# Attention scores and products with v: one TensorE block for eight heads instead of two for four, from tile 6 on

## The chip, the cores and the metric

The kernel runs on one NeuronCore of a Trainium2 chip. The metric is the device time of one execution in microseconds (us); the times shown are medians of several executions. The five engines are TensorE (PE in the profile), VectorE (DVE), ScalarE (ACT), GpSimd (POOL) and SyncE (SP, which issues the DMAs). The profile splits TensorE in two rows: PE for the matmuls and PEld for the loads of the stationary operand.

## What is computed

Three layers follow each other. The first is attention over a sliding window, the other two are dense layers on its 2304 tokens:

```python
# q, k, v: (4 batches, 8 heads, 576 positions, 64)
scores = q @ k.T / sqrt(64)
scores = where(0 <= rel < 128, scores + bias, -1e9)   # rel = position of query - position of key
attn = exp(scores - max); attn = attn / (sum + 1e-9)
x = attn @ v                       # then reshaped to (2304 tokens, 512)
g = x @ w_gate                     # 512 x 1536
x = (silu(g) * (x @ w_val)) @ w_out
h = x @ w_in                       # 512 x 2048
out = silu(h) @ w_out2             # 2304 x 512
```

The sizes are fp32. Products of the dense layers are made of a high and a low part per operand (three passes in the format `float32r` each); the products with v are done in plain fp32.

## The kernel before, in words

**Tiles and parts.** The 2304 tokens are 18 tiles of 128. Six tiles are a part, so there are three parts: tiles 0 to 5, 6 to 11, 12 to 17. For each part the kernel runs attention, then the first dense layer (`moe1`, six groups of hidden columns), then the second (`moe2`, eight groups). The attention of part 1 is spread in time over the dense layers of part 0, and that of part 2 over those of part 1 (`spread`, `attention_part`); part 2's dense layers run without attention beside them. Attention of part 0 fills the start.

**Attention of one tile.** A tile has eight heads, handled in two halves (`hf` 0 and 1) of four heads. For each half `prepare` transposes k and q on TensorE (L398, L406) and splits each into a high and a low part (tiles KR and qt). Then `attend` runs this chain: the scores on TensorE (`score`, L448) into two PSUM banks, where the two 64-row halves of the array work on a bank each; masks (L464) and bias with a row minimum (L471) on VectorE; the exponential on ScalarE (L477); the inverse of the sum on VectorE (L493, L494); the normalization on GpSimd (L497); four transposes on TensorE (L515); a copy out of PSUM (L301, tile u); two selections on GpSimd that part the weights into those of the previous tile of keys (u, L529) and those of the tile's own (l, L522); the product with v on TensorE (`weigh`, L541), whose matmuls use 64 columns of the array each; and a copy into XST (parts 1 and 2) or a split into XOP (part 0). The first tile of a batch that begins at a tile's edge (tiles 0 and 9) has only its own keys: its scores are half as wide and its product with v has half as many matmuls.

**PSUM.** There are eight banks. A group of the dense layers holds three of them as accumulators X, Y and Z while its seven products run (`quad`, L762 to L764), and blocks of the output products (`out1`, L906 to L908, and `out2`, L936 to L938) hold one each until VectorE has added it to ACC (L920, L948).

**The order.** Every operation is put into a `Plan` with a cost in ns and a due time, and `Plan.issue` simulates the engines and writes out one fixed order for each. An engine of the plan takes, of the operations whose inputs are ready, the one with the earliest due time for which enough banks are free; it does not hold banks back for an operation that needs several. Limits by kind cap the banks in use: "mm" for dense layers, "B" for operands, "S" for scores, "C" for the transposed weights, "O" for products with v, "T" for transposed k and q, "att" for the last four together. On the chip each engine then runs its list strictly in order, and waits where an input is late. `at(x)` is the due time of tile x, about 24 us apart in parts 1 and 2; the scores of a half are due at `at(i + 0.5 * hf)`, its second pair of heads and its product with v a quarter of a tile later.

**Rings.** qt has two slots (one per half), u two, l one, c two, the loaded v three (a tile's product reads the v of the tile before it too).

Of the kernel before, what the change touches and what calls it, by code (L numbers as in the profile page):

```python
# [9 lines left out]
F32 = mybir.dt.float32  # L10
# [7 lines left out]
ALU = mybir.AluOpType  # L18
PSUM = bass.MemoryType.PSUM

P = 128
# [180 lines left out]
def attention_moe_moe2_kernel(  # L202
# [33 lines left out]
    nc = tc.nc  # L236
# [7 lines left out]
    N = BT * P  # L244
    NP = H // 2
    G1, G2 = F1 // (2 * P), F2 // (2 * P)
    NU, NO, NRAW, NW, NH, NTMP = 17, 3, 2, 3, 6, 8

    big = ctx.enter_context(tc.tile_pool(name="big", bufs=1))
# [3 lines left out]
    def ring(n, shape, dtype, name):  # L253
        return [big.tile(shape, dtype, name=f"{name}{i}") for i in range(n)]
# [23 lines left out]
    QT_R = ring(2, [P, 2, 2, P], F32R, "qt")  # L278
    C_R = ring(2, [P, 4, P], F32, "c")
    ST_R = ring(2, [P, 3, 4], F32, "st")  # L280
    U_R = ring(2, [P, 4, P], F32, "u")
    L_R = ring(1, [P, 4, P], F32, "l")
    BANKS = [psp.tile([P, 512], F32, name=f"bank{i}") for i in range(8)]
    KEPT = {
        "wg": drp.tile([2 * G1, P, DM], F32, name="kept_wg"),
# [5 lines left out]
        "o2": drp.tile([2 * G2, P, 2 * DM], F32, name="kept_o2"),  # L291
    }

    plan = Plan(BANKS, {"mm": 6, "att": 4, "T": 1, "S": 3, "C": 2, "O": 1, "B": 4})

    def cost(kind, n):
        a, b = COST[kind]
# [55 lines left out]
    def first(i):  # L353
        return (i * P) % S == 0
# [66 lines left out]
        plan.add("act", cost("act_ps", 256), due, q_hi, [bq], [qk])  # L421
        plan.add("dve", cost("dve", 256), due, q_lo, [bq], [qk], give=bq)

    def attend(i, hf, dues):
        n = 2 * i + hf
        qt, qk = QT_R[n % len(QT_R)], ("qt", n % len(QT_R))
        s = i % 2
        c = 0 if first(i) else s
        cs, us, ls = n % len(C_R), n % len(U_R), n % len(L_R)
        t, st, u, lo = C_R[cs], ST_R[cs], U_R[us], L_R[ls]  # L430
        uk, lk = ("uu", us), ("l", ls)
        heads = slice(4 * hf, 4 * hf + 4)

        banks = [Bank("S"), Bank("S")]

        def score():
            for p in range(2):
                for x, y in ((0, 0), (0, 1), (1, 0)):  # L440
                    for e in range(2):
                        rows = slice(64 * e, 64 * e + 64)
                        view = banks[e].tile.rearrange("p (a b c) -> p a b c", a=2, b=2)
                        rhs = KR[rows, y, 2 * hf + p]
                        dst = view[:, p]
                        if first(i):
                            rhs, dst = rhs[:, s], dst[:, 0]
                        nc.tensor.matmul(  # L448
                            dst, qt[rows, x, p, :], rhs, start=(x == 0 and y == 0), stop=(x == 1)
                        )  # L450

        reads = [qk, ("KR", s, hf)] + ([] if first(i) else [("KR", 1 - s, hf)])
        plan.add("pe", 6 * 118 + 60, dues[0], score, reads, banks, take=tuple(banks))

        def scores(e, due):
            bank = banks[e]
            ck, stk = ("c", cs, e), ("st", cs, e)
            view = lambda: bank.tile.rearrange("p (a b c) -> p a b c", a=2, b=2)
            cur = lambda: view()[:, :, c, :]
            prev = lambda: view()[:, :, 1 - c, :]  # L460

            def mask(m, src, port):
                plan.add(
                    "dve", cost("dve", 256), due, lambda: nc.vector.copy_predicated(cur(), m, src()), [], [bank],  # L464
                    port=port,
                )

            def biased():
                for p in range(2):
                    l = 2 * p + e  # L470
                    nc.vector.tensor_tensor_reduce(  # L471
                        t[:, l, :], cur()[:, p, :], alibi[:, 4 * hf + l, :], 1.0, HUGE, ALU.add, ALU.min, st[:, 0, l:l + 1]
                    )

            def exponent():
                for l in (e, 2 + e):
                    nc.scalar.activation(  # L477
                        t[:, l, :], t[:, l, :], AF.Exp, bias=st[:, 0, l:l + 1], scale=-1.0, accum_out=st[:, 1, l:l + 1]
                    )

            mask(m_up, (lambda: bigt) if first(i) else prev, first(i))
            if not first(i) and (crossing(i) or crossing(i - 1)):
                mask(m_cross if crossing(i) else m_after, lambda: bigt, True)
            plan.add("dve", 2 * cost("dve", 136), due, biased, [bank], [ck, stk], give=bank)
            plan.add("act", 2 * (cost("act", 128) + 186), due, exponent, [], [ck, stk])

        def normalized(ps, due):
            l = slice(2 * ps[0], 2 * ps[-1] + 2)
            nl = 2 * len(ps)
            cks, stks = [("c", cs, p) for p in ps], [("st", cs, p) for p in ps]  # L490

            def invert():
                nc.vector.tensor_scalar(st[:, 2, l], st[:, 1, l], 1e-9, None, ALU.add)  # L493
                nc.vector.reciprocal(st[:, 2, l], st[:, 2, l])  # L494

            def normalize():
                nc.gpsimd.tensor_tensor(  # L497
                    t[:, l], t[:, l], st[:, 2, l].rearrange("p (a b) -> p a b", b=1).to_broadcast([P, nl, P]), ALU.mult
                )

            plan.add("dve", 290, due, invert, [], stks, port=True)
            plan.add("pool", 64 + 2.0 * nl * P, due, normalize, stks, cks)

        for e in range(2):
            scores(e, dues[e])
        normalized((0, 1), dues[1])

        due = dues[1]
        cb, ob = Bank("C"), Bank("O")
        cps = lambda: cb.tile.rearrange("p (a b) -> p a b", b=P)  # L510
        ops = lambda: ob.tile[:, 0:2 * P].rearrange("p (a b) -> p a b", b=P)

        def turn():
            for l in range(4):
                nc.tensor.transpose(cps()[:, l, :], t[:, l, :], ident)  # L515

        plan.add("pe", 4 * 109, due, turn, [("c", cs, 0), ("c", cs, 1), "ident"], [cb], take=cb)
        copy_op(512, due, lambda: u, cps, [cb], [uk], give=cb)
        if not first(i):
            plan.add(  # L520
                "pool", cost("select", 512), due,
                lambda: nc.gpsimd.affine_select(  # L522
                    lo, u, [[0, 4], [1, P]], ALU.is_ge, 0.0, base=0, channel_multiplier=-1
                ),
                [uk], [lk],
            )
            plan.add(
                "pool", cost("select", 512), due,
                lambda: nc.gpsimd.affine_select(  # L529
                    u, u, [[0, 4], [-1, P]], ALU.is_gt, 0.0, base=0, channel_multiplier=1  # L530
                ),
                [], [uk],
            )
        parts = [(i, u)] if first(i) else [(i - 1, u), (i, lo)]

        def weigh():
            for p in range(2):
                for a, (tl, m) in enumerate(parts):
                    for j in range(2):
                        l = 2 * p + j  # L540
                        nc.tensor.matmul(  # L541
                            ops()[64 * j:64 * j + 64, p, :],
                            VLD_R[tl % len(VLD_R)][:, 4 * hf + l, :],
                            m[:, l, :],
                            start=(a == 0),
                            stop=(a == len(parts) - 1),
                        )

        reads = [uk] + ([] if first(i) else [lk]) + [x for tl, _ in parts for x in loaded(tl, "v", hf)]
        plan.add("pe", 540 * len(parts) + 60, due, weigh, reads, [ob], take=ob)  # L550
        ti = i % PT
        xt = XST[:, ti, 2 * hf:2 * hf + 2, :]
        xk = [("xt", ti, 2 * hf + p) for p in range(2)]
        if i >= PT:
            copy_op(256, due, lambda: xt, ops, [ob], xk, give=ob)
        else:
            slot, t0 = x_slot(hf, ti // BT), (ti % BT) * P
            xh, xl = XOP[:, slot, 0, :, t0:t0 + P], XOP[:, slot, 1, :, t0:t0 + P]
            keys = [("X", slot, kk, ti % BT) for kk in range(2)]
            copy_op(256, due, lambda: xh, ops, [ob], keys)  # L560
            plan.add(
                "dve", cost("dve", 256), due,
                lambda: nc.vector.tensor_tensor(xl, ops(), xh.bitcast(F32), ALU.subtract), [ob], keys, give=ob,  # L563
            )


# [399 lines left out]
    def attention_part(part, at):  # L966
        for i in range(part * PT, part * PT + PT):
            load(i, "k", at(i) - 14820.0)
            load(i, "q", at(i) - 20070.0)
            load(i, "v", at(i) - 7670.0)  # L970
            for hf in range(2):
                prepare(i, hf, at(i + 0.5 * hf) - 8000.0)
                attend(i, hf, [at(i + p / NP) for p in (2 * hf, 2 * hf + 1)])

    def ramp(x):
        return 5000.0 + 6130.0 * min(x, 1) + 10170.0 * min(max(x - 1, 0), 1) + 7700.0 * max(x - 2, 0)
# [124 lines left out]
```

## Time and profile before

| | |
|---|---|
| median of 3 executions | 954.29 us (953.21 to 955.04) |
| profiled execution | 954.24 us, span of its instructions 952.5 us |
| TensorE, matmuls | busy 931.7 us, 98% |
| VectorE, ScalarE, GpSimd | busy 68%, 52%, 37% |
| mean granted TensorE clock | 0.998 of 2.4 GHz |

The profile's times are us from the first instruction of that execution; the 1.7 us between span and time lie outside of it. Matmuls overlap: one record's duration is a latency, and what a matmul costs the engine is the distance between its start and the start of the next one. A name such as "L448" is a line of the kernel; one matmul instruction in plain fp32 shows as two records (L541).

### The profile page before, as it was taken

How to read it: one execution, taken by the hardware profiler on the slowest of the kernel's cores; microseconds unless marked ns; L12 is line 12 of the kernel's file. 1: busy time of each engine (PE TensorE's matmuls, PEld its weight loads, DVE VectorE, ACT ScalarE, POOL GpSimd, SP SyncE). 2: the span in 40 equal slices, each digit the busy share in tenths (PEclk: the TensorE clock that was granted, in tenths of full speed). 3: DMA queues.
4: the chain of work that ended last, by engine and by line, in shares of the span. 5: the costliest groups of instructions: out<-in, count | busy, mean ns of one | idle time of the engine just before them, and what ended most of it. 6: DMA issues, size and time to landing. Idle time of an engine off the chain costs nothing.

```text
span 952.5 us, 16827 instructions
## 1 busy us (share of the span) xinstructions
PE 931.7 (98%) x5662; PEld 854.8 (90%) x5662; DVE 644.8 (68%) x1489; ACT 499.2 (52%) x1269; POOL 352.9 (37%) x426
## 2 busy tenths in 40 slices
PE   7999999998999999999999999999999999999998
PEld 5888989998887888999999998888899999988886
DVE  7886666758798889557666756657745555855655
ACT  6877555556866765665453564345343323553331
POOL 2645333347666788796651521111200000300000
PEclk9999999999999999999999999999999999999999
DMA  9978897776578987998766666355466666654522
GB/s 216 276 240 253 271 301 260 256 241 207 189 255 262 293 266 259 362 285 287 227 200 185 198 201 191 125 167 184 162 239 201 208 214 215 204 198 170 161 89 89
DMA packets 156854, 209.78 MB, mean 220 GB/s; under 512 B 65760, under 2 KB 86496, under 8 KB 156768
## 3 DMA queue, kind: packets, MB, share of 16 engines
q1 hardware_dynamic: 156768, 208.71, 68.2%
q8 instruction: 45, 0.74, 0.3%
q14 instruction: 41, 0.34, 0.1%
HBM read 146.28 MB, written 62.39 MB: 219 GB/s over the span
## 4 chain that ended last, share of the span: by engine, by line
PE 86%; DVE 7%; DMA 3%; ACT 2%; POOL 1%; issue 1%; SPq 0%; DVEq 0%; ACTq 0%; POOLq 0%
PE bank L762 15%; PE bank L763 14%; PE bank L764 14%; PE bank L936 6%; PE bank L938 6%; PE bank L937 6%; PE bank L906 5%; PE bank L907 5%; PE bank L908 5%; PE bank L448 3%; PE bank L541 3%; DVE word L663 2%; PE bank L515 1%; DMA raw<-in_moe_w_in_dram 1%; DVE bank L464 1%
## 5 line engine op out<-in xcount | busy, mean ns | idle before, releaser
L762 PE MATMUL bank<-XOP,wu 128*128 128x384 f32 (+2 forms) x880 | 301.5, 343 | 6.7 <-DVE qt L412 2.1
L763 PE MATMUL bank<-XOP,wu 128*128 128x384 f32 (+2 forms) x880 | 293.8, 334 | 0.6 <-DVE XOP L563 0.5
L764 PE MATMUL bank<-XOP,wu 128*128 128x384 f32 (+2 forms) x880 | 294.0, 334 | 0.1
L762 PEld LDWEIGHTS bank<-XOP,wu 128*128 128x128 f32 x880 | 165.5, 188 | 15.9 <-ACT tmp L301 2.8
L763 PEld LDWEIGHTS bank<-XOP,wu 128*128 128x128 f32 x880 | 165.8, 188 | 2.2 <-DVE XOP L563 0.7
L764 PEld LDWEIGHTS bank<-XOP,wu 128*128 128x128 f32 x880 | 165.6, 188 | 0.4 <-POOL wu L311 0.4
L311 POOL TENSOR_TENSOR h<-tmp,h 128x384 fp32r<-128x384 f32 x67 | 71.3, 1074 | 194.7 <-ACT h L301 186.4
L301 ACT ACTIVATE tmp<-bank 128x384 f32<-128x384 f32 x140 | 65.5, 489 | 108.1 <-PE bank L764 73.3
L936 PE MATMUL bank<-wo,h 128*128 128x512 f32 x290 | 116.1, 400 | 0.5 <-DVE ACC L948 0.5
L938 PE MATMUL bank<-wo,h 128*128 128x512 f32 x290 | 114.0, 393 | 0.0
L937 PE MATMUL bank<-wo,h 128*128 128x512 f32 x290 | 113.9, 393 | 0.0
L948 DVE TENSOR_TENSOR ACC<-bank,ACC 128x512 f32<-128x512 f32 (+1 forms) x127 | 86.0, 682 | 32.5 <-PE bank L938 32.0
L865 DVE SCALAR_TENSOR_TENSOR tmp<-tmp,bank 128x384 f32<-128x384 f32 (+2 forms) x128 | 68.6, 544 | 53.4 <-ACT tmp L855 43.7
L906 PE MATMUL bank<-h,wo 128*128 128x384 f32 (+2 forms) x296 | 100.9, 341 | 0.0
L907 PE MATMUL bank<-h,wo 128*128 128x384 f32 (+2 forms) x296 | 98.5, 333 | 0.6 <-POOL h L311 0.6
L908 PE MATMUL bank<-h,wo 128*128 128x384 f32 (+2 forms) x296 | 98.6, 333 | 0.0
L802 DVE TENSOR_TENSOR bank<-bank,tmp 128x384 f32<-128x384 f32 x96 | 53.8, 561 | 52.9 <-PE bank L764 41.1
L301 ACT ACTIVATE h<-tmp 128x384 fp32r<-128x384 f32 x102 | 52.5, 521 | 61.3 <-PE bank L937 35.2
L920 DVE TENSOR_TENSOR ACC<-bank,ACC 128x384 f32<-128x384 f32 x120 | 65.3, 553 | 22.8 <-PE bank L908 22.5
L855 ACT ACTIVATE tmp<-bank 128x384 f32<-128x384 f32 (+2 forms) x134 | 63.2, 482 | 32.7 <-PE bank L764 19.4
L311 POOL TENSOR_TENSOR wu<-word,wu 128x256 fp32r<-128x256 f32 x69 | 52.3, 775 | 61.9 <-ACT wu L301 47.4
L497 POOL TENSOR_TENSOR c<-c,st 128x512 f32<-128x512 f32 x36 | 39.1, 1087 | 93.6 <-DVE st L494 91.1
(98 smaller groups left out, 1580.5 us busy)
## 6 DMA issues: line engine op xcount, KB each, us to landing
wo<-kept_o SPq DMA_DIRECT2D x56, 512.0 KB, 4.1
wu<-kept_i SPq DMA_DIRECT2D x112, 256.0 KB, 3.6
wu<-kept_g SPq DMA_DIRECT2D x60, 256.0 KB, 3.6
wu<-kept_v SPq DMA_DIRECT2D x60, 256.0 KB, 3.9
raw<-in_moe_w_out_dram SPq DMA_DIRECT2D x28, 512.0 KB, 4.6
kept_o<-wo SPq DMA_DIRECT2D x28, 512.0 KB, 3.8
kept_i<-wu SPq DMA_DIRECT2D x56, 256.0 KB, 2.9
kept_g<-wu SPq DMA_DIRECT2D x42, 256.0 KB, 4.3
```

The costliest lines, as they stand in the source:

```text
L301: act = lambda: nc.scalar.activation(out(), src(), AF.Copy)
L311: pool = lambda: nc.gpsimd.tensor_tensor(out(), x(), y(), op)
L762: nc.tensor.matmul(ps, wh, xh, start=start, stop=False, skip_group_check=True)
L763: nc.tensor.matmul(ps, wh, xl, start=False, stop=False, skip_group_check=True)
L764: nc.tensor.matmul(ps, wl, xh, start=False, stop=stop, skip_group_check=True)
L906: nc.tensor.matmul(ps[:, 0:n], wh, h[:, 0], start=(i == 0), stop=False)
L907: nc.tensor.matmul(ps[:, 0:n], wh, h[:, 1], start=False, stop=False)
L908: nc.tensor.matmul(ps[:, 0:n], wl, h[:, 0], start=False, stop=(i == 1))
L936: nc.tensor.matmul(ps, hh, wh, start=(i == 0), stop=False)
L937: nc.tensor.matmul(ps, hh, wl, start=False, stop=False)
L938: nc.tensor.matmul(ps, hl, wh, start=False, stop=(i == 1))
L948: plan.add("dve", cost("dve", n), due, lambda: nc.vector.tensor_tensor(acc, pv(), acc, ALU.add), [b], keys, give=b)
```

## The change

From tile 6 on (`EARLY = 6`), `score` and `weigh` are each planned as one TensorE operation for both halves: 24 score matmuls into four banks that are taken together, and 32 records of product with v (16 at tile 9) into one bank, which is then copied to XST by one copy of 512 columns instead of two of 256. Tiles 0 to 5 keep one operation per half. `prepare` of both halves of a merged tile is now due with the tile. Masks, exponentials, normalization, transposes and selections remain per half with their due times. The limits go from att 4, S 3 to att 6, S 4; u has three slots and l two. The costs that the planner uses for the TensorE operations change for all tiles: scores from 768 ns per half to 708 ns per half plus 290 ns, products with v from 1140 ns per half (two groups of keys) to 436 ns per half plus 290 ns.

```diff
+    EARLY = 6
-    U_R = ring(2, [P, 4, P], F32, "u")
-    L_R = ring(1, [P, 4, P], F32, "l")
+    U_R = ring(3, [P, 4, P], F32, "u")
+    L_R = ring(2, [P, 4, P], F32, "l")
-    plan = Plan(BANKS, {"mm": 6, "att": 4, "T": 1, "S": 3, "C": 2, "O": 1, "B": 4})
+    plan = Plan(BANKS, {"mm": 6, "att": 6, "T": 1, "S": 4, "C": 2, "O": 1, "B": 4})
-    def attend(i, hf, dues):
+    def score(i, halves, due):
+        s = i % 2
+        banks = {hf: (Bank("S"), Bank("S")) for hf in halves}
+        def products():
+            for hf in halves:
+                qt = QT_R[(2 * i + hf) % len(QT_R)]
+                for p in range(2):
+                    for x, y in ((0, 0), (0, 1), (1, 0)):
+                        for e in range(2):
...
+        reads = [("qt", (2 * i + hf) % len(QT_R)) for hf in halves]
+        reads += [("KR", t, hf) for t in ((s,) if first(i) else (s, 1 - s)) for hf in halves]
+        take = tuple(b for hf in halves for b in banks[hf])
+        plan.add("pe", 6 * 118 * len(halves) + 290, due, products, reads, list(take), take=take)
+        return banks
...
-        plan.add("pe", 6 * 118 + 60, dues[0], score, reads, banks, take=tuple(banks))
...
+    def weigh(i, halves, due):
+        ob = Bank("O")
+        ops = lambda hf: ob.tile.rearrange("p (a b) -> p a b", b=P)[:, 2 * hf:2 * hf + 2]
...
-        plan.add("pe", 540 * len(parts) + 60, due, weigh, reads, [ob], take=ob)
+        plan.add("pe", 218 * len(halves) * (1 if first(i) else 2) + 290, due, product, reads, [ob], take=ob)
...
+                if last and len(halves) == 2:
+                    all_k = [("xt", ti, c) for c in range(KC)]
+                    copy_op(
+                        512, due, lambda: XST[:, ti], lambda: ob.tile.rearrange("p (a b) -> p a b", b=P), [ob], all_k, give=ob
+                    )
...
-            for hf in range(2):
-                prepare(i, hf, at(i + 0.5 * hf) - 8000.0)
-                attend(i, hf, [at(i + p / NP) for p in (2 * hf, 2 * hf + 1)])
+            for halves in [(0,), (1,)] if i < EARLY else [(0, 1)]:
+                t0 = at(i + 0.5 * halves[0])
+                for hf in halves:
+                    prepare(i, hf, t0 - 8000.0)
+                banks = score(i, halves, t0)
+                for hf in halves:
+                    attend(i, hf, [at(i + p / NP) for p in (2 * hf, 2 * hf + 1)], banks[hf])
+                weigh(i, halves, at(i + 0.5 * halves[-1] + 1 / NP))
```

## Rows read from the trace of the kernel before

**Rows 1.** The page, busy us of each engine, share of the span, instructions.

```profile
PE 931.7 (98%) x5662; PEld 854.8 (90%) x5662; DVE 644.8 (68%) x1489; ACT 499.2 (52%) x1269; POOL 352.9 (37%) x426
```

**Rows 2.** Busy time by stretch: length, engines, granted clock, DMA share, GB/s.

```profile
0.00:60.00 60.00, 53.26 (x488) 44.89 (x490) 48.16 (x201) 44.87 (x155) 25.59 (x37) 1.00 0.91 242
60.00:391.00 331.00, 322.22 (x1975) 292.25 (x1974) 251.03 (x551) 211.35 (x533) 192.38 (x229) 0.99 0.79 259
391.00:689.00 298.00, 297.21 (x1812) 272.53 (x1811) 190.24 (x454) 149.21 (x388) 121.59 (x147) 1.00 0.64 207
```

**Rows 3.** TensorE's waits from 60 to 675 us: total, times, longest.

```profile
PE bank L762 <- DVE qt L412: 2.1, 1, 2.1
...
PE bank L541 <- POOL u L529: 1.6, 1, 1.6
...
PE bank L448 <- DVE qt L412: 0.6, 1, 0.6
```

**Rows 4.** TensorE's groups by form: scores and products with v; count, busy us, mean ns.

```profile
L448 PE MATMUL bank<-KR,qt 64*128 64x256 f32 x384 | 32.8, 304 | 1.3 <-ACT KR L301 0.7 <-DVE qt L412 0.6
L541 PE MATMUL bank<-u,vld 128*64 128x128 f32 x288 | 29.5, 289 | 2.3 <-POOL u L529 1.6 <-ACT u L301 0.6
```

**Rows 5.** TensorE in order of time around one score block: start, us, instruction.

```profile
316.06 0.40 PE L938 MATMUL bank<-wo,h 128*128 128x512 f32 x1
316.39 0.95 PE L448 MATMUL bank<-KR,qt 64*128 64x256 f32 x12
317.27 0.45 PE L762 MATMUL bank<-XOP,wu 128*128 128x384 f32 x1
317.55 0.34 PE L763 MATMUL bank<-XOP,wu 128*128 128x384 f32 x1
317.73 0.33 PE L764 MATMUL bank<-XOP,wu 128*128 128x384 f32 x1
```

**Rows 6.** The matmuls of that block which are running at 316.90 us.

```profile
316.72 0.39 PE L448 MATMUL bank<-KR,qt 64*128 64x256 f32 x4
```

**Rows 7.** TensorE in order of time around one product with v.

```profile
288.91 0.40 PE L938 MATMUL bank<-wo,h 128*128 128x512 f32 x1
289.24 0.44 PE L541 MATMUL bank<-u,vld 128*64 128x128 f32 x4
289.51 0.39 PE L541 MATMUL bank<-l,vld 128*64 128x128 f32 x4
...
289.94 0.39 PE L541 MATMUL bank<-l,vld 128*64 128x128 f32 x4
290.26 0.50 PE L936 MATMUL bank<-wo,h 128*128 128x512 f32 x1
290.60 0.39 PE L937 MATMUL bank<-wo,h 128*128 128x512 f32 x1
290.83 0.40 PE L938 MATMUL bank<-wo,h 128*128 128x512 f32 x1
```

**Rows 8.** TensorE where a product with v of tile 9 meets a score block.

```profile
268.28 0.66 PE L541 MATMUL bank<-u,vld 128*64 128x128 f32 x8
268.87 0.97 PE L448 MATMUL bank<-KR,qt 64*128 64x256 f32 x12
```

**Rows 9.** All engines in order of time, 508 to 536 us: one score block's banks, one output block.

```profile
510.83 0.97 PE L448 MATMUL bank<-KR,qt 64*128 64x256 f32 x12
...
512.10 0.42 DVE L464 COPY_PREDICATED bank<-m_up,bank 128x256 f32<-128x256 uint8 x1
...
515.06 0.28 DVE L471 CUSTOM_DVE_ANT_0 c<-bank,alibi 128x128 f32<-128x128 f32 x1
...
518.42 0.34 PE L908 MATMUL bank<-h,wo 128*128 128x384 f32 x1
...
518.79 0.56 DVE L920 TENSOR_TENSOR ACC<-bank,ACC 128x384 f32<-128x384 f32 x1 [0.38 <-PE bank L908]
```

**Rows 10.** One short stretch after waits: length, engines, clock, DMA share, GB/s.

```profile
238.00:241.50 3.50, 3.50 (x18) 3.00 (x16) 3.14 (x7) 2.44 (x6) 1.01 (x1) 0.52 0.45 176
```

More of the change, by code (lines that the diff above doesn't have):

```diff
@@ L422, in prepare, with attend @@
         plan.add("dve", cost("dve", 256), due, q_lo, [bq], [qk], give=bq)
-    def attend(i, hf, dues):
+    def score(i, halves, due):
[7 more added lines that the diff above has]
+                        for e in range(2):
+                            rows = slice(64 * e, 64 * e + 64)
+                            view = banks[hf][e].tile.rearrange("p (a b c) -> p a b c", a=2, b=2)
+                            rhs, dst = KR[rows, y, 2 * hf + p], view[:, p]
+                            if first(i):
+                                rhs, dst = rhs[:, s], dst[:, 0]
+                            nc.tensor.matmul(
+                                dst, qt[rows, x, p, :], rhs, start=(x == 0 and y == 0), stop=(x == 1)
+                            )
[4 more added lines that the diff above has]
+        return banks
+    def attend(i, hf, dues, banks):
         n = 2 * i + hf
-        qt, qk = QT_R[n % len(QT_R)], ("qt", n % len(QT_R))
         s = i % 2
@@ L431, in attend @@
         uk, lk = ("uu", us), ("l", ls)
[L432 to L452, printed above, removed]
-        plan.add("pe", 6 * 118 + 60, dues[0], score, reads, banks, take=tuple(banks))
         def scores(e, due):
@@ L508, in attend @@
         due = dues[1]
-        cb, ob = Bank("C"), Bank("O")
+        cb = Bank("C")
         cps = lambda: cb.tile.rearrange("p (a b) -> p a b", b=P)
-        ops = lambda: ob.tile[:, 0:2 * P].rearrange("p (a b) -> p a b", b=P)
         def turn():
@@ L533, in attend @@
             )
[L534 to L547, printed above, removed]
@@ L549, in attend, with product @@
-        reads = [uk] + ([] if first(i) else [lk]) + [x for tl, _ in parts for x in loaded(tl, "v", hf)]
-        plan.add("pe", 540 * len(parts) + 60, due, weigh, reads, [ob], take=ob)
-        ti = i % PT
[L552 to L556, printed above, removed]
+    def weigh(i, halves, due):
+        ob = Bank("O")
+        ops = lambda hf: ob.tile.rearrange("p (a b) -> p a b", b=P)[:, 2 * hf:2 * hf + 2]
+        parts, reads = {}, []
+        for hf in halves:
+            us, ls = (2 * i + hf) % len(U_R), (2 * i + hf) % len(L_R)
+            parts[hf] = [(i, U_R[us])] if first(i) else [(i - 1, U_R[us]), (i, L_R[ls])]
+            reads += [("uu", us)] + ([] if first(i) else [("l", ls)])
+            reads += [x for tl, _ in parts[hf] for x in loaded(tl, "v", hf)]
+        def product():
+            for hf in halves:
+                for p in range(2):
+                    for a, (tl, m) in enumerate(parts[hf]):
+                        for j in range(2):
+                            l = 2 * p + j
+                            nc.tensor.matmul(
+                                ops(hf)[64 * j:64 * j + 64, p, :],
+                                VLD_R[tl % len(VLD_R)][:, 4 * hf + l, :],
+                                m[:, l, :],
+                                start=(a == 0),
+                                stop=(a == len(parts[hf]) - 1),
+                            )
+        plan.add("pe", 218 * len(halves) * (1 if first(i) else 2) + 290, due, product, reads, [ob], take=ob)
+        ti = i % PT
+        for n, hf in enumerate(halves):
+            last = hf == halves[-1]
+            xk = [("xt", ti, 2 * hf + p) for p in range(2)]
+            if i >= PT:
+                if last and len(halves) == 2:
+                    all_k = [("xt", ti, c) for c in range(KC)]
+                    copy_op(
+                        512, due, lambda: XST[:, ti], lambda: ob.tile.rearrange("p (a b) -> p a b", b=P), [ob], all_k, give=ob
+                    )
+                elif len(halves) == 1:
+                    copy_op(256, due, lambda: XST[:, ti, 2 * hf:2 * hf + 2], lambda: ops(hf), [ob], xk, give=ob)
+                continue
@@ L559, in attend @@
             keys = [("X", slot, kk, ti % BT) for kk in range(2)]
-            copy_op(256, due, lambda: xh, ops, [ob], keys)
+            copy_op(256, due, lambda xh=xh, hf=hf: xh, lambda hf=hf: ops(hf), [ob], keys)
             plan.add(
                 "dve", cost("dve", 256), due,
-                lambda: nc.vector.tensor_tensor(xl, ops(), xh.bitcast(F32), ALU.subtract), [ob], keys, give=ob,
+                lambda xl=xl, xh=xh, hf=hf: nc.vector.tensor_tensor(xl, ops(hf), xh.bitcast(F32), ALU.subtract),
+                [ob] + [("ob", i, h) for h in halves[:n]], keys + [("ob", i, hf)], give=ob if last else None,
             )
@@ L970, in attention_part @@
             load(i, "v", at(i) - 7670.0)
-            for hf in range(2):
-                prepare(i, hf, at(i + 0.5 * hf) - 8000.0)
-                attend(i, hf, [at(i + p / NP) for p in (2 * hf, 2 * hf + 1)])
+            for halves in [(0,), (1,)] if i < EARLY else [(0, 1)]:
+                t0 = at(i + 0.5 * halves[0])
+                for hf in halves:
+                    prepare(i, hf, t0 - 8000.0)
+                banks = score(i, halves, t0)
+                for hf in halves:
+                    attend(i, hf, [at(i + p / NP) for p in (2 * hf, 2 * hf + 1)], banks[hf])
+                weigh(i, halves, at(i + 0.5 * halves[-1] + 1 / NP))
     def ramp(x):
```

## Prediction

> **What bounds the kernel now.** I read the page first, then busy time by stretch, TensorE's waits, and TensorE's matmuls in order of time around single attention blocks. The page shows TensorE busy for 98% of the span while VectorE, ScalarE and GpSimd stand at 68%, 52% and 37% [rows 1]. By stretch this is tighter where the change acts: from 60 to 391 us TensorE works 322.22 of 331 us, from 391 to 689 us 297.21 of 298 [rows 2]. So in parts 1 and 2 the end is set by how long TensorE's own list is, and a microsecond taken out of that list is a microsecond of the kernel, unless it comes back as a wait. But "busy" hides something: a matmul's record is a latency, so an engine that drains between two kinds of block still counts as busy. Only distances between starts show that, and the change is about these.
>
> **What a block costs beyond its matmuls.** A score block first. The last matmul ahead of it starts at 316.06 and the block at 316.39, 0.33 us later [rows 5]; between two neighbours of that width with nothing between them the distance is 290.83 − 290.60 = 0.23 [rows 7]. So 0.10 is lost going in. The block takes 317.27 − 316.39 = 0.88 until the next matmul starts. Its twelve matmuls run in pairs, one per half of the array: at 316.90 the oldest that still run began at 316.72 [rows 6], which is 0.33 after the first pair, or three pairs at 0.11. Six pairs are 0.66, so 0.22 of the 0.88 is no matmul's. Going out, the first dense matmul is followed after 317.55 − 317.27 = 0.28, where 317.73 − 317.55 = 0.18 is usual: another 0.10 [rows 5]. A score block pays 0.10 + 0.22 + 0.10 = 0.42 us beside its 0.66.
>
> A product with v: going in 289.24 − 288.91 − 0.23 = 0.10; four groups of four records take 290.26 − 289.24 = 1.02, and in the middle two groups take 289.94 − 289.51 = 0.43, so four are 0.86 and 0.16 is no matmul's; going out 290.60 − 290.26 − 0.23 = 0.11 [rows 7]. That is 0.37 per block. Tile 9 is a check on this split: half the records, 268.87 − 268.28 = 0.59 [rows 8], where half of 0.86 plus 0.16 also gives 0.59. The fixed part does not shrink with the block.
>
> **The change part by part.**
>
> *Score blocks.* 432 matmuls of twelve per block are 36 blocks, two for each of 18 tiles; the 384 of full width among them are 32 blocks [rows 4], the other four those of tiles 0 and 9. Twelve tiles (6 to 17) have their two blocks made one: 12 × 0.42 = 5.0 us less. No matmul is saved; the second half's six pairs follow in the same arrangement of the array, and in a block nothing is seen to be paid between its pairs p = 0 and p = 1.
>
> *Products with v.* 288 records on u, eight per block, are again 36 blocks [rows 4]; 12 × 0.37 = 4.4 us less.
>
> Bounds of these two: nothing, if what surrounds a block is paid again between the halves (the rows speak against it), and 9.4 us together. Where blocks already lie side by side, as in [rows 8], the going-in and going-out are shared in part, so 9.4 is the upper end. I take it whole: I saw only this one place where a product meets a score block directly from tile 6 on.
>
> *Copies to XST.* Two of 256 columns become one of 512. They are ScalarE's, which is busy for 211 of 331 and 149 of 298 us in these stretches [rows 2]: hidden, no gain. If that cover were gone, the wider copy would only hold one bank longer.
>
> *Waits of TensorE.* From 60 to 675 us its attention blocks waited 1.6 us for a selection and 0.6 us for a qt [rows 3], 2.2 us in all for the 48 score blocks and products of tiles 6 to 17, 0.046 each. A merged block waits for both halves, and so for the later of two chains; behind it in TensorE's list stand the dense matmuls, which then wait as well. Below, the 24 merged blocks could wait for nothing and give back 2.2. Above, twice the chains and twice the banks at 0.046 × 4 are 0.18 each, 4.4 in all, a loss of 2.2. I take half of that, +1.1, because the planner sees these chains and the due time of the product stays where the second half's was.
>
> *The planner's costs.* The new price of a merged product with v is 872 + 290 = 1162 ns, where the rows give 8 × 0.215 + 0.37 = 2.1 us; before it was 1140 for a half that takes 1.23. So TensorE runs later than planned by some 0.9 us per tile for that, about as before (two halves at 0.09 and two score blocks at 1.08 against 768 ns, 0.8 together). A TensorE that is late against its plan makes others wait for it, which costs nothing. I take zero.
>
> *Tiles 0 to 5.* Their operations stay, but new costs, limits and rings reorder the start, where TensorE is idle 6.7 of 60 us and the DMA engines are 91% busy [rows 2]. Both ends are bounded by that idle time: some of it won, or as much again lost. Loads set the pace there, and they do not change; I take zero and keep ±3.
>
> *Waits that the new order may move.* The longest wait in the stretch, 2.1 us for a VectorE queue, lies where VectorE makes the operands of the second layer [rows 3], and a spell of half clock follows: 0.52 granted from 238 to 241.5 us, after those idle gaps [rows 10]. It costs about half of 3.5 us, 1.7. A new order can lose this wait and its slow spell (−3.8) or get a second one (+3.8). I take zero.
>
> **The sum.** 954.24 of the profiled execution (0.05 under the median, so no correction) − 5.0 − 4.4 + 1.1 = **945.9 us**.
>
> **Rivals.**
>
> *Slower: four banks at once leave the dense layers too few.* A score block's two banks are held from 510.83 to 515.06 + 0.28 = 515.34, 4.5 us [rows 9], because VectorE empties them one after the other between its other work. Four would be held some 9 us. For that long four banks are left, and a running group holds three; its output blocks then follow each other through one bank. One such block's last matmul starts at 518.42, so the next could start at 518.59, but its bank is read by VectorE until 518.79 + 0.56 = 519.35 [rows 9]: 0.76 us of idle TensorE each. This decides from one such block per tile: 12 × 0.76 = 9.1 takes the gain back. With two per tile 18.2 are lost, and the time is 954.2 − 9.4 + 18.2 = 963. For it: the plan holds no banks back, it fits the score block in where four happen to be free. Against it: VectorE has a quarter to a third of these stretches idle, X, Y and Z of one group are emptied soon after its end, and in the trace before no long wait of an output block shows. The Trainium skill speaks for this rival ("Perfetto Trace Analysis", Optimization Strategy): the same gap repeating on the engine that should be saturated can mean that there isn't enough PSUM for the next tile. No such gap is in the trace before; after, it would be one near each score block.
>
> *No change.* Either one such stalled block per tile, or the cost between halves is paid inside the block as it was outside: 954. Against the latter stands tile 9, where the fixed part stays out of the inner groups.
>
> *More gained.* The gain stands whole, waits shrink by 2.2 and the wait with its slow spell goes: 954.2 − 9.4 − 2.2 − 3.8 = 939.
>
> **How the numbers follow.** Forecast (942.5 to 949.5): 0.62. Slower, 963: 0.22. No change, 954: 0.11. More gained, 939: 0.05. A measurement of this kernel tells about 0.2% (1.9 us) from no change; so below 952.4 is faster: 0.62 + 0.05, and a little of the case of no change that falls just short of it, 0.68; within 0.2%: 0.10; slower: 0.22. The range reaches from 941.5 (the forecast's low end with some of the slow spell gone) up through the no-change case to 957; the slower case above that and little else stay out, about 0.2.
>
> **What the profile after would show.** Right: 24 records in a score block taking 12 × 0.11 + 0.22 = 1.54 us to the next start, a product with v of 8 × 0.215 + 0.16 = 1.88, twelve of each from tile 6 on, TensorE's busy time down by about 9 us, and its idle time within 3 us of the 20.8 now. Wrong in size: 0.2 or more between the halves inside a block. Wrong in sign: TensorE's idle time up by 9 us or more, with output blocks or first matmuls of a group waiting for VectorE or ScalarE right behind score blocks; or longer waits in the second layer's operands near 236 us, with more of the half clock.

## The result, and the profile after

The changed kernel takes 946.74 us (median of 6 executions, 941.25 to 949.25) against 954.56 of the kernel before in the same comparison: a ratio of 0.9918 with a 95% interval of 0.9893 to 0.9944. The forecast was 945.9. The profiled execution, 941.25 us, is the quickest of its kernel; a second profile of the same kernel (below) took 948.09.

The page of the changed kernel, and its busy time by stretch (length, TensorE's matmuls and loads, VectorE, ScalarE, GpSimd, clock, DMA share, GB/s), which answer to [rows 1, 2]:

```profile
span 939.2 us, 16809 instructions
...
PE 920.8 (98%) x5662; PEld 853.4 (91%) x5662; DVE 636.1 (68%) x1484; ACT 496.1 (53%) x1253; POOL 363.0 (39%) x435
```

```profile
60.00:391.00 331.00, 323.76 (x2027) 298.96 (x2024) 250.87 (x566) 214.84 (x544) 198.85 (x236) 1.00 0.81 268
391.00:689.00 298.00, 297.19 (x1826) 277.08 (x1826) 190.30 (x440) 147.33 (x370) 122.33 (x148) 1.00 0.63 210
```

TensorE's busy time fell from 931.7 to 920.8 us with the same 5662 matmuls, and its idle time from 20.8 to 939.2 − 920.8 = 18.4. Its matmuls in order of time around a merged score block, and around a merged product with v:

```profile
308.85 0.39 PE L965 MATMUL bank<-wo,h 128*128 128x512 f32 x1
309.17 1.64 PE L447 MATMUL bank<-KR,qt 64*128 64x256 f32 x24
310.74 0.45 PE L789 MATMUL bank<-XOP,wu 128*128 128x384 f32 x1
311.02 0.34 PE L790 MATMUL bank<-XOP,wu 128*128 128x384 f32 x1
```

```profile
301.56 0.44 PE L561 MATMUL bank<-u,vld 128*64 128x128 f32 x4
301.83 0.39 PE L561 MATMUL bank<-l,vld 128*64 128x128 f32 x4
...
302.27 0.39 PE L561 MATMUL bank<-l,vld 128*64 128x128 f32 x4
302.48 0.39 PE L561 MATMUL bank<-u,vld 128*64 128x128 f32 x4
...
303.46 0.44 PE L407 MATMUL bank<-ident,qld 128*128 128x128 f32 x2
```

The score block takes 310.74 − 309.17 = 1.57 us, where two of [rows 5] took 1.76 and went in and out twice. The product takes 303.46 − 301.56 = 1.90; between the halves (302.27 to 302.48, 0.21) nothing is lost: that is the ordinary distance within a block. TensorE's waits from 60 to 675 us (total, times, longest), which answer to [rows 3]:

```profile
PE bank L789 <- DVE tmp L844: 2.8, 2, 2.3
PE bank L789 <- ACT tmp L302: 2.5, 5, 1.1
PE bank L789 <- DVE XOP L311: 1.2, 1, 1.2
```

No attention block waits in this stretch any more. What waits is L789, the first matmul of a dense product, for the copies and sums of its group's accumulators (L302, L844) and for an operand (L311).

### The profile page after: what moved, and what is told of

Its sections match the earlier page's. It is cut to its first block, busy times and chain, and to the rows that moved or that the text cites. A ratio compares the mean times of both kernels' runs of the same rounds, so it can differ in the third digit from the quotient of the medians.

```text
span 939.2 us, 16809 instructions
## 1 busy us (share of the span) xinstructions
PE 920.8 (98%) x5662; PEld 853.4 (91%) x5662; DVE 636.1 (68%) x1484; ACT 496.1 (53%) x1253; POOL 363.0 (39%) x435
## 4 chain that ended last, share of the span: by engine, by line
PE 82%; DVE 9%; POOL 2%; ACT 2%; issue 2%; DMA 1%; SPq 0%; DVEq 0%; POOLq 0%; ACTq 0%
PE bank L789 14%; PE bank L790 14%; PE bank L791 14%; PE bank L963 6%; PE bank L965 6%; PE bank L964 6%; PE bank L933 5%; PE bank L934 5%; PE bank L935 5%; PE bank L447 3%; PE bank L561 3%; PE bank L524 2%; DVE word L690 1%; DVE bank L632 1%; DVE XOP L311 1%
## 5 line engine op out<-in xcount | busy, mean ns | idle before, releaser
L789 PE MATMUL bank<-XOP,wu 128*128 128x384 f32 (+2 forms) x880 | 300.3, 341 | 8.3 <-DVE tmp L844 2.8
L789 PEld LDWEIGHTS bank<-XOP,wu 128*128 128x128 f32 x880 | 165.3, 188 | 17.1 <-ACT tmp L302 4.8
L302 ACT ACTIVATE tmp<-bank 128x384 f32<-128x384 f32 x141 | 66.1, 489 | 107.0 <-PE bank L791 70.9
L302 ACT ACTIVATE h<-tmp 128x384 fp32r<-128x384 f32 x101 | 52.0, 521 | 60.4 <-PE bank L964 34.6
L690 DVE SCALAR_TENSOR_TENSOR word<-raw,top 128x512 int32<-128x512 int32 x68 | 56.1, 824 | 22.0 <-ACT top L687 16.4
```

The lines of the kernel that those rows point to most:

```text
L302: act = lambda: nc.scalar.activation(out(), src(), AF.Copy)
L789: nc.tensor.matmul(ps, wh, xh, start=start, stop=False, skip_group_check=True)
```

## The experiments

Theory A: the gain is the 24 drains that are not paid, and it is there in every order. Theory B: the gain is another order with other waits. All ratios are to the kernel before, in the same comparison.

| kernel | median us | ratio, 95% interval |
|---|---|---|
| e1_again, the changed kernel | 944.94 | 0.9925 (0.9900 to 0.9950) |
| e2_switch_between | 952.45 | 1.0012 (0.9991 to 1.0032) |
| e3_same_arrangement | 944.62 | 0.9918 (0.9898 to 0.9938) |
| e4_never_merged | 947.69 | 0.9958 (0.9936 to 0.9980) |
| e5_costs_only | 949.85 | 0.9968 (0.9949 to 0.9988) |
| e6_scores_merged | 959.63 | 1.0067 (1.0042 to 1.0092) |
| e7_products_merged | 948.43 | 0.9969 (0.9944 to 0.9994) |
| e8_price_right | 943.55 | 0.9917 (0.9886 to 0.9947) |
| e9_part2_merged | 945.88 | 0.9944 (0.9925 to 0.9962) |
| e10_seven_banks_merged | 948.12 | 0.9959 (0.9944 to 0.9975) |
| e11_seven_banks_halves | 962.32 | 1.0106 (1.0080 to 1.0131) |
| e12_part2_price | 951.25 | 0.9996 (0.9977 to 1.0015) |

The kernel before measured 951.93 us beside e1 to e4, 952.01 beside e5 to e8, 951.47 beside e9 to e12.

**The changed kernel again.** No edit.

> The changed kernel unaltered, for a second profile. The first profiled execution took 941.25 us, 5.5 under the median of its runs, and shows no spell of half clock after the start. Theory A (the gain is 24 drains saved, 9.2 us, in every execution; what varies is the clock): 946 to 948 us, TensorE's blocks again 1.58 and 1.90 us, and a spell of half clock near the wait in the second layer's operands (some 226 to 231 us), costing about 1.7 us each. Theory B (the gain is a luckier order of waits): the blocks are the same but the waits of TensorE add up to several us more or less than the 18.4 us of the first profile, without a change in clock.

944.94 us, and the profiled execution 948.09, with the same blocks. The two profiles of one program differ by 6.8 us of span. Busy time by stretch, the first profile:

```profile
20.00:27.00 7.00, 6.37 (x67) 4.73 (x65) 5.98 (x24) 6.57 (x27) 5.39 (x7) 1.00 1.03 280
```

and the second:

```profile
20.00:27.00 7.00, 6.77 (x44) 5.01 (x46) 4.56 (x19) 5.65 (x21) 4.85 (x7) 0.51 1.05 300
...
276.00:279.50 3.50, 1.57 (x10) 1.25 (x9) 3.43 (x6) 1.09 (x2) 2.95 (x3) 1.00 0.39 154
279.50:283.00 3.50, 3.50 (x11) 3.50 (x12) 2.16 (x4) 2.01 (x6) 1.01 (x1) 0.51 0.99 279
```

In the second, TensorE works at a clock of 0.51 (the 1.2 GHz level) from 20 to 27 us, doing 44 matmuls where the first does 67; and again after a wait of 1.93 us at 279.5. The first dense matmul starts at 25.31 us in the first profile and at 28.41 in the second, so the start makes 3 us of the difference; the spell at 279.5 costs about 1.7 by estimate (half of 3.5). The clock is the larger part of what varies, as theory A had it. But its range for the time is missed by 1 us, its spell came after another wait than the one named, and waits differ too: TensorE is idle for 946.0 − 926.1 = 19.9 us here, against 18.4.

**One drain put back, in the same order.** Every engine's list is that of the changed kernel; TensorE's has 24 transposes of the identity more.

```diff
             for hf in halves:
                 qt = QT_R[(2 * i + hf) % len(QT_R)]
+                if hf != halves[0]: nc.tensor.transpose(banks[hf][0].tile[:, 0:P], ident, ident)
...
             for hf in halves:
+                if hf != halves[0]: nc.tensor.transpose(ops(hf)[:, 0], ident, ident)
```

> The changed kernel with every engine's order as it is, and one 128x128 transpose of the identity put between the two halves of each merged block (24 in all, into a bank region that the second half overwrites). Theory A: the array changes its arrangement twice more per block, so a score block pays 0.42 us again and a product with v 0.37, and each transpose itself some 0.06: 12 x (0.42 + 0.37 + 0.12) = 10.9 us more than the changed kernel, 956 to 959, all of the gain gone. Theory B: only the transposes' own time, 24 x 0.06 = 1.4 us more, some 948.

952.45 us, 7.5 above the changed kernel and level with the kernel before. TensorE around one score block and one product with v of this kernel:

```profile
582.88 0.96 PE L447 MATMUL bank<-KR,qt 64*128 64x256 f32 x12
583.78 0.33 PE L438 MATMUL bank<-ident 128*128 128x128 f32 x1
584.03 0.96 PE L447 MATMUL bank<-KR,qt 64*128 64x256 f32 x12
584.93 0.45 PE L789 MATMUL bank<-XOP,wu 128*128 128x384 f32 x1
```

```profile
572.07 0.44 PE L561 MATMUL bank<-u,vld 128*64 128x128 f32 x4
...
573.09 0.33 PE L556 MATMUL bank<-ident 128*128 128x128 f32 x1
573.35 0.44 PE L561 MATMUL bank<-u,vld 128*64 128x128 f32 x4
...
574.37 0.44 PE L407 MATMUL bank<-ident,qld 128*128 128x128 f32 x2
```

The score block takes 584.93 − 582.88 = 2.05 us, 0.48 more than merged; the product with v takes 574.37 − 572.07 = 2.30, 0.40 more, the transpose itself included in both. Twelve tiles make 10.6 us of TensorE's list, as theory A expected (10.9). The medians differ by 7.5, all of the gain, far from theory B's 1.4; the two intervals leave room for 4 to 12.5, so the medians alone don't tell 7.5 from the whole.

**Work put between, without a switch.** The same places, but matmuls in the block's own arrangement.

```diff
+                for e in range(2 if hf != halves[0] else 0): nc.tensor.matmul(banks[hf][e].tile[:, 0:2 * P]..., qt[64 * e:64 * e + 64, 0, 0, :], KR[64 * e:64 * e + 64, 0, 2 * hf], start=True, stop=True)
...
+                for j in range(2 if hf != halves[0] else 0): nc.tensor.matmul(ops(hf)[64 * j:64 * j + 64, 0, :], VLD_R[i % len(VLD_R)][:, 4 * hf + j, :], parts[hf][-1][1][:, j, :], start=True, stop=True)
```

> The control to the run with transposes: the order is kept again, and what is put between the halves are matmuls in the block's own arrangement (one more pair of score matmuls of 0.11 us, one more pair of products with v of 0.215 us, overwritten by the second half). Both theories: 12 x (0.11 + 0.215) = 3.9 us more than the changed kernel, some 951, and no gap inside the blocks. If an interruption of any kind costs what the switch is said to cost, it is 10 us or more.

944.62 us, 0.3 under the changed kernel. The score block of this kernel:

```profile
575.15 0.95 PE L447 MATMUL bank<-KR,qt 64*128 64x256 f32 x12
575.94 0.28 PE L438 MATMUL bank<-KR,qt 64*128 64x256 f32 x2
576.05 0.84 PE L447 MATMUL bank<-KR,qt 64*128 64x256 f32 x12
576.82 0.45 PE L789 MATMUL bank<-XOP,wu 128*128 128x384 f32 x1
```

It takes 1.67 us, 0.10 more than merged and without a gap: so the 0.48 above is the switch's, not that of any interruption. But 12 × 0.325 = 3.9 us of added work leave the median where it was, some 6 us under what both theories expected. Where the work went is read below, with the cuts of e4.

**No merging, new costs, limits and rings.** `EARLY = 18`. This also gives `prepare` of the second half its old due time and makes two copies to XST again.

> The change without its merging (no tile has its halves as one block), with the new costs, limits and rings. Theory A: the 9.2 us are lost again and the time is that of the kernel before within 3 us, 952 to 957. Theory B (costs, limits and rings make the better order): about that of the changed kernel, 944 to 949.

947.69 us: 4.2 under the kernel before, with not one drain saved. Theory A's number fails and theory B's range holds: 4.2 of the 7.0 us by which e1 is under the kernel before come without merging. Against the changed kernel 2.8 us are left for the merging, and the two intervals overlap: by the medians alone it is not clear of noise. The profiles say where it went. This kernel, in two stretches with the same dense matmuls (the 301st to the 1531st, and on to the 3001st, of 4398 in one fixed count):

```profile
95.71:366.57 270.86, 266.59 (x1623) 241.91 (x1623) 207.75 (x445) 173.68 (x425) 164.93 (x190) 1.00 0.79 259
366.57:680.24 313.67, 313.38 (x1903) 287.42 (x1902) 205.85 (x483) 159.88 (x414) 140.34 (x171) 1.00 0.66 213
```

and the changed kernel between the same matmuls:

```profile
95.74:363.94 268.20, 261.61 (x1611) 241.08 (x1611) 201.36 (x426) 171.98 (x418) 160.77 (x188) 1.00 0.80 263
363.94:675.31 311.37, 309.98 (x1901) 287.41 (x1900) 205.40 (x483) 158.20 (x408) 142.00 (x173) 1.00 0.64 212
```

TensorE's busy time is 5.0 and 3.4 us less; 0.9 of that is one score block (12 matmuls of the 1623) that the merged order has done before the first cut, so 7.5 are saved. Its idle time goes from 270.86 − 266.59 = 4.27 to 6.59 and from 0.29 to 1.39: of 7.5 us taken out of TensorE's work, 3.4 come back as waits and 4.1 stay.

Here too busy time hides something. One of the changed kernel's waits:

```profile
379.88 0.34 PE L791 MATMUL bank<-XOP,wu 128*128 128x384 f32 x1
380.80 0.44 PE L789 MATMUL bank<-XOP,wu 128*128 128x384 f32 x1 [0.58 <-DVE st L481]
381.08 0.34 PE L790 MATMUL bank<-XOP,wu 128*128 128x384 f32 x1
```

The idle time is 0.58 us, but the start comes 0.92 after the last one where 0.17 is usual, and the next one 0.28 after it where 0.18 is usual: 0.85 are lost, and 0.27 of them count as busy. So the blocks save more, and the waits take more, than busy and idle time say.

The second profile of the changed kernel, between the same matmuls:

```profile
98.41:370.35 271.94, 263.55 (x1612) 242.53 (x1612) 202.54 (x426) 171.26 (x418) 160.68 (x188) 0.99 0.80 260
370.35:682.23 311.88, 310.24 (x1901) 287.35 (x1900) 206.10 (x483) 158.28 (x408) 142.17 (x173) 1.00 0.66 212
```

Its first stretch, with the spell at 279.5 us and 8.4 us of idle time, is no shorter than that of e4. So the 4.1 us are those of the quickest execution; in the other one only the second stretch is shorter, by 1.8.

The same cuts in e2, and then in e3, whose orders are the changed kernel's:

```profile
98.91:369.78 270.87, 266.18 (x1623) 243.03 (x1623) 199.46 (x426) 172.50 (x418) 161.83 (x188) 1.00 0.81 261
369.78:686.69 316.91, 315.60 (x1914) 289.43 (x1912) 206.90 (x483) 158.56 (x408) 142.21 (x173) 1.00 0.64 209
```

```profile
95.62:363.65 268.03, 263.44 (x1645) 243.00 (x1645) 198.11 (x426) 171.52 (x416) 160.55 (x186) 1.00 0.81 263
363.65:677.79 314.14, 312.46 (x1938) 289.25 (x1936) 207.11 (x483) 158.26 (x408) 143.73 (x174) 1.00 0.65 210
```

Against the first profile of the changed kernel, in the second stretch all of the added work arrives: busy 5.6 and 2.5 us more, length 5.5 and 2.8 more (5.0 and 2.3 against the second profile). In the first stretch 4.6 and 1.8 us of busy time lengthen it by 2.7 and −0.2, and the idle time falls from 6.6 to 4.7 and 4.6. The wait of 2.32 us at 297.30 us for a sum on VectorE (L844) is what has gone: in the first stretches of e2 and of e3 that line reads

```profile
PE bank L789 <- DVE tmp L844: 0.5, 1, 0.5
```

where the changed kernel has 2.8, 2, 2.3. So TensorE's list is the bound, as the prediction had it, in the second stretch; in the first, part of a change in its length is taken up by its waits.

**The planner's costs alone.** As e4, with the rings, att and S of before.

```diff
-    U_R = ring(3, [P, 4, P], F32, "u")
-    L_R = ring(2, [P, 4, P], F32, "l")
+    U_R = ring(2, [P, 4, P], F32, "u")
+    L_R = ring(1, [P, 4, P], F32, "l")
...
```

> Nothing merged, and limits (att 4, S 3) and rings (u 2, l 1) as before; of the change only the planner's new costs of score blocks and products with v are left. The run without merging but with new costs, limits and rings gave 947.69 against 951.93 us of the kernel before. Theory C (the costs alone make that gain): 946 to 949 us. Theory D (the third u, the second l and the wider limits make it, since a product waits less for its slot): 950.5 to 953, as before.

949.85 us, between the two theories. New prices make about 2 us (ratio 0.9968, clear of 1); rings and limits perhaps 2 more, but the intervals of e5 and e4 overlap, so that part is not shown.

**One of the two merged.** In e6 the product stays per half, in e7 the scores. In e6 `prepare` of both halves is still due with the tile; in e7 that of the second half has its old due time.

```diff
+                for one in [(hf,) for hf in halves]: weigh(i, one, at(i + 0.5 * one[0] + 1 / NP))   # e6
...
+            for halves in [(0,), (1,)]:                                                             # e7
...
+                if i < EARLY or halves == (1,): weigh(i, halves if i < EARLY else (0, 1), at(i + 0.5 * halves[-1] + 1 / NP))
```

> New costs, limits and rings; from tile 6 on the scores of both halves are one block in four banks, but the products with v stay one per half, due as in the kernel before. Drains alone: 947.7 - 12 x 0.42 = 942.7. The run with transposes between the halves showed that the merged order loses some 3.3 us beside its drains. Theory E (taking four banks at once loses them): 945 to 947 here, and all of 947.7 - 4.4 = 943.3 in the run with merged products. Theory F (the product that waits for the later of two chains loses them): 942 to 943.5 here, and 945.5 to 947 there.

> New costs, limits and rings; the scores stay one block per half in two banks, from tile 6 on the products with v of both halves are one block. Drains alone: 947.7 - 12 x 0.37 = 943.3. Theory E (four banks at once lose 3.3 us): 942.5 to 944. Theory F (the later of two chains loses them): 945.5 to 947.

959.63 and 948.43 us. Neither theory holds: with the scores merged alone the kernel is slower than before, merging products alone gains nothing over e4, and both together are better than either. The parts don't add up. TensorE's waits of e6 from 60 to 675 us:

```profile
PE bank L561 <- POOL u L538: 4.4, 2, 2.8
PE bank L965 <- POOL h L312: 3.1, 1, 3.1
PE bank L789 <- DVE tmp L892: 2.2, 1, 2.2
```

Products with v wait for their selections again, one for 2.8 us; and the mean clock of its executions is 0.989 to 0.994, where those of the kernel before beside them have 0.996 to 1.000. Why this order waits so much stays open; the due time of `prepare` is one difference to e7 that no run takes by itself.

**The right price.** `218 * len(halves)` becomes `436 * len(halves)`.

> The changed kernel, but the planner's cost of a product with v is what the trace shows: 436 ns per half and group of keys (872 in the kernel before 540 x 2) plus 290, instead of 218. The prediction gave this price no effect: within 1.5 us of the changed kernel, 943.5 to 946.5. Theory C (costs are what orders the waits): another time by 2 us or more, either way, with TensorE's idle time other than 16 to 20 us.

943.55 us, 1.4 under the changed kernel, not clear of it. The prediction's number holds. Its profile has 947.5 − 925.0 = 22.5 us of idle time, outside of 16 to 20 as theory C had it, but that execution (949.19 us) is the slowest of its kernel and speaks little for the others.

**Merged in part 2 alone**, `EARLY = 12`, with the old price (e9) and the right one (e12).

> New costs, limits and rings, blocks per half up to tile 11 and merged ones for tiles 12 to 17 alone. Up to about 370 us every engine's order is that of the run without merging. Theory G (the drains are saved wherever blocks are merged, and what the merged order costs lies in part 1, at the operands and in the raw weights' stage): the run without merging less 6 x 0.79 = 4.7 us, 947.7 - 4.7 = 943.0, no more than the changed kernel, and TensorE ahead of the run without merging by 4 to 5 us at 690 us with the same start. Theory H (each new order draws its waits anew, merging saves nothing reliable): anywhere from 945 to 955, with waits in part 2 that eat the drains.

> Merged blocks for tiles 12 to 17 alone, and the planner's cost of a product with v as the trace shows it (436 ns per half and group of keys). Theory G: as with merged blocks in part 2 alone and the old price within 2 us, 941 to 945. Theory H: off by more than 2 us either way.

945.88 and 951.25 us. Neither is faster than the changed kernel. Between the 1531st and the 3001st dense matmul e9 takes 312.1 us and e12 313.1, where the unmerged e4 takes 313.7 and the merged kernels 311.4, 311.9 (e1) and 311.1 (e8): part 2 gains 0.6 to 2.6 of the 4.7 us of its drains. Theory G is too high, and theory H, with the price as a mere reshuffle, is what e12 shows.

**Seven banks.** `for i in range(7)` in BANKS, merged (e10) and with `EARLY = 18` (e11).

> The changed kernel with one PSUM bank less (seven), so that a merged score block leaves three to the dense layers. The rival of the prediction (four banks at once leave too few): 12 tiles with two or more output blocks of 0.76 us idle each, so 18 us or more above the changed kernel, 963 or more, with first matmuls of a group or output blocks waiting right behind score blocks. If banks are not near their limit: within 5 us, 942 to 950.

> The control: seven banks and no merging. If the lost bank itself hurts the dense layers, this is as much above the run without merging (947.7) as the merged one is above the changed kernel. The rival: a score block takes only two banks here, so within 4 us, 945 to 952, and well under the merged run with seven banks.

948.12 and 962.32 us. With three banks left to the dense layers beside a score block, the merged kernel loses 3.2 us, not 18, inside the other expectation (942 to 950). The rival of four banks is out. Neither expectation had the 14.6 that the unmerged kernel loses; its TensorE waits 4.1 us once for VectorE near 363 us and 2.9 once for ScalarE near 345, each followed by a spell of half clock, and why its order has them stays open.

## Why the prediction came out right

**The drains: right, term by term.** Score block 1.54 us forecast, 1.57 measured; product 1.88 and 1.90; nothing between the halves. By the distances shown a merged tile saves (1.76 − 1.57 + 0.20) + (2.04 − 1.90 + 0.21) = 0.74 us, twelve of them 8.9, where 9.4 was forecast. The Trainium skill says ("TensorEngine Tiling (Array Packing)", Key Properties) that changing the tiling mode drains TensorE. The runs with work between the halves agree and put a number to it: 0.48 and 0.40 us for a round trip with a transpose, none without a switch.

**That all of it reaches the end: wrong.** The sum took 9.4 us as the kernel's. With the order held, all of a change in TensorE's list arrives in the second stretch and 2.7 of 4.6 (e2) or nothing of 1.8 (e3) in the first. Against an unmerged kernel of the same costs 4.1 of 7.5 us of busy time arrive in the quicker profile, and 2.8 by the medians. The rest becomes waits at the dense layers' own first matmuls, for copies and sums on ScalarE and VectorE.

**Waits, +1.1: the place was wrong.** The merged attention blocks of the first profile wait for nothing, not for the later of two chains. The loss lies in the dense matmuls and is 3.4 us of idle time, more by distances.

**Costs, limits and rings at zero: wrong.** They gain about 4 us by themselves (e4; 2 to 6 by its interval). Here the prediction reasoned that a TensorE which lags its plan costs nothing, and overlooked that prices also decide what the plan puts next to what. It had a price for it all the same, taken at zero: a new order can lose the wait of 2.1 us with its spell of half clock, 3.8 us. In e4's profile that wait is gone and the clock stays at 1.00; its largest waits from 60 to 675 us are

```profile
PE bank L561 <- POOL u L538: 2.5, 3, 1.3
PE bank L789 <- DVE tmp L844: 1.7, 3, 0.6
```

That this is most of the 4.2 fits, but no run isolates it.

**The sum came out by luck.** It put −9.4 + 1.1 + 0 = −8.3 us. The runs show −7.5 of TensorE's busy time, 3.4 of waits that the merging brings and −4.2 of costs, limits and rings, which is −8.3 too. The misses cancel, and the forecast of 945.9 is better than its reasons.

**The rivals.** The four banks were tried and are out at eight banks, and at seven. The last read of the score block shown above is

```profile
315.55 0.29 DVE L481 CUSTOM_DVE_ANT_0 c<-bank,alibi 128x128 f32<-128x128 f32 x1
```

so its banks were held for 315.84 − 309.17 = 6.7 us, not 9, and no wait of TensorE lies in that time. "No change" had the cost paid again between the halves, and 0.21 us between them leaves nothing of it. "More gained" at 939 resembles the quickest execution (941.25), in which no spell of half clock follows the start.

**What stays open.** Which part of a new order makes the waits. With eight banks, versions that differ only in prices, ring sizes or in what is merged spread from 943.6 us (e8) to 959.6 (e6), and the effects of single edits don't add up. None is shown better than the changed kernel: e8 and e3 are level with it. What the merging alone is worth against e4 is not clear of noise either.

## What to carry to other kernels

On TensorE read distances between starts, not busy time: a block in another arrangement of the array here costs 0.4 us beside its matmuls, which busy time hides, and putting two such blocks together saved it in TensorE's list. A wait, too, cost more than its idle time. In a kernel whose order comes from a planner, test an edit with the order held (put the cost back in place, add work beside it) before believing its time: replanning alone moved this kernel by several us either way. And read by stretch what arrives: where TensorE hardly waited (1.4 of 311 us) a change in its list came through whole, where it waited more (6.6 of 268 us) about half of it or nothing did.

## What was not expected of the hardware

Executions of one and the same program differ by a spell of half clock near the start: 0.51 from 20 to 27 us in one profile, 1.00 in another, 3 us apart at the first dense matmul. Later spells follow some single waits and not others. With a spell behind them: 1.93 us at 279.5 in e1, 2.07 at 236.8 in the kernel before, 2.75 at 169.8 and 3.11 at 365.6 in e6. Without one: 2.32 at 297.3 in the first profile of the changed kernel, 2.30 at 284.0 in e5, 2.31 at 281.5 in e10. So the length of a wait alone doesn't tell here whether a spell follows. A spell of 3.5 us costs about 1.7 us on top of the wait by estimate; the last one of e6 is longer and costs about 3:

```profile
365.50:372.00 6.50, 6.41 (x27) 4.71 (x28) 3.81 (x6) 0.46 (x2) 2.92 (x4) 0.52 1.01 345
```
